# Five head pairs held to the program's order, copies moved behind maxima, and the first weight words on GpSimd's queue

## The chip, the cores and the metric

One core of a Trainium2 chip runs the whole program. The metric is the device time of one execution in microseconds; lower is better. TensorE (PE) multiplies into PSUM, VectorE (DVE) and ScalarE (ACT) read PSUM and work element by element, GpSimd (POOL) works on SBUF only. DMAs are issued from the queues of SyncE (SP), ScalarE and GpSimd.

## The reference: attention, then two feed-forward layers

```python
scores = scale * np.matmul(q, k.transpose(0, 1, 3, 2))      # q, k, v: 4 x 8 heads x 576 x 64
bias = -(cum[:, :, :, None] - cum[:, :, None, :])           # cum: running sum of max(s, 0)
scores = np.where(causal, -1000000000.0, scores + np.minimum(bias, 0.0))
scores = scores - np.max(scores, axis=-1, keepdims=True)
attn = np.exp(scores)
attn = attn / (np.sum(attn, axis=-1, keepdims=True) + 1e-09)
x = np.matmul(attn, v)                                      # then as 2304 tokens x 512
h = x @ w_in;  x = np.maximum(h, 0.0) ** 2 @ w_out          # 512 -> 2048 -> 512
h = x @ w2_in; return np.maximum(0.01 * h, h) @ w2_out      # once more, with a leaky ReLU
```

The weights arrive as 64-bit floats. The kernel takes them as pairs of 32-bit words and puts float32 values together from them.

## The kernel before

Attention runs in 16 pairs of heads. Each pair passes through seven slots, the pieces of `STEPS`: tiles of kind 0 (128 and 384 keys together), 2, 3 and 4 (the last 64 rows of both heads), for kinds 0, 2 and 3 once for each head of the pair. The loop in `attention` walks over slots y = 7x + st. In a slot it emits first the row maxima (`maxima`, VectorE) and the exponentials (`exponentials`, ScalarE, which also sums the rows into `sums`). Then come the TensorE instructions: transposes of a finished kind into PSUM (`flip`, two slots behind its exponentials), the product with v (`values`, for columns below 256 and above), and the scores of a kind to come (`scores`). `flip` also emits the copies of the transposed tiles out of PSUM into `pT` and `pX`: on ScalarE for kinds 0 and 2, on VectorE for kinds 3 and 4. PSUM has four `tr` banks for transposes and products, two `S` and two `h` banks for scores. Next come `gather` (product out of PSUM into `xo`), `inverse` (reciprocal of the sums on VectorE, spread over 64 columns by GpSimd into `ex`), `spread` (its transpose on TensorE) and `scale` (VectorE), each at a fixed slot count k0 after its pair began. For the first five pairs (`ALONE`, `PLAIN`) `scale` is done in two portions, columns 0 to 255 (a = 0) and the rest (a = 2).

Side work hangs on slots through `at_slot`: loads of q, k (`load_qk`), v (`load_v`, three buffers) and the bias rows (`load_bias`); `turn`, which transposes q and k on VectorE; `last_rows` on GpSimd; and `load_w`, which fetches one of the 16 column chunks of the first weight matrix (512 KB of words, `wst`, two buffers, on SyncE's queue) and three slots later has ScalarE (L114, L115), VectorE (L117, L120) and GpSimd (L122) put the words together, and then writes the chunk as a rounded part (ScalarE L169) and a rest (GpSimd L172). A chunk starts every two and a half slots from slot 11 on. From slot 35 on (`START[0]`) the matrix products of the first layer (`up1`) are filled in between attention's own TensorE work.

The order in which each engine gets its instructions is decided by a list scheduler with modelled times, except where `in_order` chains the instructions of an engine as they were written. Before, that chain covers TensorE from slot 35 on, and within single groups. Every engine then works through its queue strictly in that order. After attention two further layers follow in blocks of 768 tokens, mainly TensorE work.

Of the kernel before, what the change touches and what calls it, by code (L numbers as in the profile page):

```python
# [23 lines left out]
def attention_then_two_mlps(  # L24
# [24 lines left out]
    nc = tc.nc  # L49
# [108 lines left out]
    def load_w(fc, pool, stage, lo_engine=nc.gpsimd):  # L158

        st = stage.words()  # L160
        read_w(st, w1_in, fc, False)
        for _ in range(3):
            yield
        dst = pool.tile([P, 2, DM], F32R, tag=f"w{fc}", name=f"w{fc}")
        win[fc] = dst
        t = stage.word()
        yield from words(t, st)
        if fc < 10:
            nc.scalar.activation(dst[:, 0], f32(t), AF.Copy)  # L169
        else:  # L170
            nc.vector.tensor_copy(dst[:, 0], f32(t))
        lo_engine.tensor_tensor(dst[:, 1], f32(t), f32(dst[:, 0]), ALU.subtract)  # L172
# [193 lines left out]
    class Pair:  # L366


        def __init__(self, b, g, i):
            self.b, self.g, self.i = b, g, i  # L370
            self.h = [4 * g + 2 * e + i for e in range(2)]
            self.pT, self.sc, self.po = {}, {}, {}

# [142 lines left out]
    def flip(at, x, kind, ts):  # L516
# [19 lines left out]
        for r in range(2):  # L536
# [6 lines left out]
            else:  # L543
                jobs.append((p.pT[1][:, 1 - r, :, 2 * P:], src[:, 0, 0:4]))
                jobs.append((p.pX[:, r], src[:, 0, 4]))
        for out, src in jobs:
            if kind > 2:
                nc.vector.tensor_copy(out, src)
            else:
                nc.scalar.activation(out, src, AF.Copy)  # L550

# [119 lines left out]
    def attention(at, mg, mx):  # L671
# [65 lines left out]
        for x in range(len(pairs)):  # L737
# [8 lines left out]
            if x + 2 < len(pairs):  # L746
                if x and x % 2 == 0:
                    at_slot(y + 3, load_qk, at, x + 2)
                at_slot(y + 5, load_v, at, x + 2)

# [7 lines left out]
        for fc in range(FC):  # L758
            job = load_w(fc, wpool, stage)
            for gap in range(6):  # L760
                at_slot(CV + 5 * fc // 2 + (4 if fc > 7 else 0) + gap, step, job)
# [48 lines left out]
        for y in range(end + 14):  # L810
            x, st = divmod(y, n)
            if y == START[0]:
                fixed_from = len(nc.cur_bb.bb.instructions)
            if y < end:
                args = maxima(at, x, *STEPS[st])
                live[y] = args[0]
                behind = [args[-1], exponentials(*args[:-1])]
            fill(y, 0)
            tiled = len(nc.cur_bb.bb.instructions)
# [22 lines left out]
            for px in (x - 1, x):  # L842
# [8 lines left out]
                for when, a, b in portions:  # L851
                    if k0 == when:
                        scale(px, a, b)
                    if k0 == when - 4:
                        inverse(at, px, a, b)
                    if k0 == when - 1:
# [318 lines left out]
```

## Time and profile before

| | us |
|---|---|
| median of three runs | 930.9 |
| fastest run | 930.15 |
| profiled execution, its own time | 932.79 |
| its span, first to last instruction | 931.0 |
| TensorE busy | 898.3 (96%) |
| VectorE busy | 705.7 (76%) |
| ScalarE busy | 577.7 (62%) |
| GpSimd busy | 179.9 (19%) |

The profiled execution is 1.9 us above the median. Busy TensorE time is modelled for matmuls that overlap, so it tells where TensorE has work, not how well it is used. The mean granted clock of TensorE is 0.996 of full speed. Slots 0 to 34, the five pairs of the change, lie in the first 78 us of the span.

### The profile page before, as it was taken

How to read it: one execution, taken by the hardware profiler on the slowest of the kernel's cores; microseconds unless marked ns; L12 is line 12 of the kernel's file. 1: busy time of each engine (PE TensorE's matmuls, PEld its weight loads, DVE VectorE, ACT ScalarE, POOL GpSimd, SP SyncE). 2: the span in 40 equal slices, each digit the busy share in tenths (PEclk: the TensorE clock that was granted, in tenths of full speed). 3: DMA queues.
4: the chain of work that ended last, by engine and by line, in shares of the span. 5: the costliest groups of instructions: out<-in, count | busy, mean ns of one | idle time of the engine just before them, and what ended most of it. 6: DMA issues, size and time to landing. Idle time of an engine off the chain costs nothing.

```text
span 931.0 us, 16390 instructions
## 1 busy us (share of the span) xinstructions
PE 898.3 (96%) x5902; PEld 809.0 (87%) x5902; DVE 705.7 (76%) x1286; ACT 577.7 (62%) x1076; POOL 179.9 (19%) x290
## 2 busy tenths in 40 slices
PE   5878999999999999999999999999999999999997
PEld 3646777777777778999999999999999999999997
DVE  5888776876774267589897997787488697886964
ACT  4788876878886444365565556686577754444442
POOL 4357763344330001001112101001110000000000
PEclk9999999999999999999999999999999999999999
DMA  9776849778763377948649326668768575627303
GB/s 164 172 184 153 217 145 230 219 204 245 227 203 106 99 239 274 316 163 269 228 132 363 128 96 201 218 221 304 256 205 299 187 254 149 182 57 208 86 13 55
DMA packets 229569, 178.48 MB, mean 192 GB/s; under 512 B 139600, under 2 KB 206352, under 8 KB 229488
## 3 DMA queue, kind: packets, MB, share of 16 engines
q1 hardware_dynamic: 192568, 105.13, 41.7%
q10 hardware_dynamic: 27048, 38.16, 11.3%
q0 software_dynamic: 9872, 34.15, 10.5%
q8 instruction: 46, 0.75, 0.3%
q14 instruction: 35, 0.29, 0.1%
HBM read 111.25 MB, written 66.13 MB: 191 GB/s over the span
## 4 chain that ended last, share of the span: by engine, by line
PE 53%; issue 13%; DVE 6%; DMA 6%; POOL 1%; ACT 1%; POOLq 0%; ACTq 0%; DVEq 0%; SPq 0%
PE q L877 30%; PE h L661 16%; DVE op L984 3%; PE tr L569 2%; DMA gp<-gscr 2%; PE S L469 2%; PE tr L527 1%; PE S L457 1%; DMA gp<-qscr 1%; DMA wst<-in_moe_w_in_dram 1%; DMA qscr<-post 1%; DVE gp L978 1%; DMA wst<-in_moe_w_out_dram 1%; DVE wt L119 0%; POOL zscr L1046 0%
## 5 line engine op out<-in xcount | busy, mean ns | idle before, releaser
L877 PE MATMUL q<-op,w 128*128 128x384 f32 x3024 | 527.9, 335 | 4.0 <-DVE op L984 2.7
L877 PEld LDWEIGHTS q<-op,w 128*128 128x128 f32 x3024 | 523.7, 188 | 7.9 <-DVE op L984 5.0
L983 ACT ACTIVATE op<-gp 128x768 fp32r<-128x768 f32 x189 | 158.3, 846 | 152.3 <-PE q L877 128.4
L661 PE MATMUL h<-xs,w 128*128 128x512 f32 (+1 forms) x960 | 211.5, 374 | 1.2 <-ACT gs L640 0.8
L984 DVE TENSOR_TENSOR op<-gp,op 128x768 fp32r<-128x768 f32 x189 | 178.0, 953 | 40.6 <-ACT op L983 39.4
L661 PEld LDWEIGHTS h<-xs,w 128*128 128x128 f32 x960 | 163.6, 189 | 38.0 <-issue 6.0
L512 ACT ACTIVATE t<-t,m 128x256 f32<-128x256 f32 (+4 forms) x134 | 76.1, 569 | 44.1 <-DVE m L488 39.2
L488 DVE CUSTOM_DVE_ANT_0 t<-S,mask 128x128 f32<-128x128 f32 (+4 forms) x119 | 49.5, 460 | 43.3 <-PE S L469 28.2
L640 ACT ACTIVATE gs<-h 128x512 f32<-128x512 f32 (+1 forms) x80 | 43.8, 549 | 47.3 <-PE h L661 46.8
L185 POOL DMA_DIRECT2D wscr<-wt x48 | 26.6, 555 | 231.2 <-DVE wt L120 227.4
L950 DVE TENSOR_TENSOR post<-q,post 128x768 f32<-128x768 f32 (+1 forms) x55 | 51.6, 940 | 15.1 <-PE q L877 14.7
L469 PE MATMUL S<-Y 64*128 64x128 f32 (+3 forms) x324 | 42.9, 372 | 14.0 <-DVE Y L427 8.0
L930 ACT ACTIVATE post<-q 128x768 f32<-128x768 f32 (+1 forms) x56 | 43.8, 782 | 12.6 <-PE q L877 12.5
L114 ACT ACTIVATE wt<-wst 128x512 f32<-128x512 f32 x64 | 42.3, 661 | 12.2 <-DMA wst<-in_moe_w_in_dram 5.9
L569 PE MATMUL tr<-pT,v 128*64 128x320 f32 (+3 forms) x384 | 46.8, 387 | 2.5 <-ACT pT L550 2.0
L120 DVE SCALAR_TENSOR_TENSOR wt<-wst,wt 128x512 uint32<-128x512 uint32 x64 | 48.1, 753 | 0.9
L527 PEld LDWEIGHTS tr<-ident,t 64*128 64x128 f32 x720 | 28.6, 140 | 20.5 <-issue 11.3
L910 ACT ACTIVATE post<-post 128x768 f32<-128x768 f32 x36 | 30.4, 846 | 25.5 <-DVE post L950 25.4
L117 DVE TENSOR_SCALAR wt<-wt 128x512 uint32<-128x512 uint32 x64 | 31.7, 496 | 18.2 <-ACT wt L114 18.1
L569 PEld LDWEIGHTS tr<-pT,v 128*64 128x64 f32 x384 | 24.9, 137 | 23.1 <-issue 4.2
L115 ACT ACTIVATE wst<-wst 128x512 uint32<-128x512 uint32 x64 | 42.9, 670 | 2.7 <-DMA wst<-in_moe_w_out_dram 1.8
L198 DVE TENSOR_TENSOR w<-wq,w 128x512 fp32r<-128x512 f32 x49 | 33.3, 688 | 14.2 <-ACT w L197 13.9
(119 smaller groups left out, 943.7 us busy)
## 6 DMA issues: line engine op xcount, KB each, us to landing
gscr<-gs ACTq DMA_DIRECT2D x36, 512.0 KB
gp<-gscr SPq DMA_DIRECT2D x48, 384.0 KB
qscr<-post ACTq DMA_DIRECT2D x48, 384.0 KB
gp<-qscr SPq DMA_DIRECT2D x48, 384.0 KB
wscr<-wt POOLq DMA_DIRECT2D x48, 256.0 KB, 4.5
wst<-in_moe_w_in_dram SPq DMA_DIRECT2D x19, 512.0 KB
wst<-in_moe_w_out_dram SPq DMA_DIRECT2D x16, 512.0 KB
wst<-in_moe_w_out_dram POOLq DMA_DIRECT2D x16, 512.0 KB, 5.1
```

What stands on the lines that cost most here:

```text
L120: nc.vector.scalar_tensor_tensor(t, hw, 0xC0000000, t, ALU.bitwise_and, ALU.bitwise_or)
L469: nc.tensor.matmul(p.sc[kind][e][:, a:z], qs[hs, T * P:(T + 1) * P], ks[hs, :z - a], start=(n == 0 and y == 0), stop=(n == len(tiles) - 1 ...
L488: return nc.vector.tensor_tensor_reduce(t[:, a:z], sc, msk, -QK_SCALE, first, ALU.add, ALU.min, m).ins
L512: done = nc.scalar.activation(t[:, a:z], t[:, a:z], AF.Exp, bias=m[:, c:c + 1], scale=-1.0, accum_out=sums[:, s0:s0 + 1])
L569: p.anchor = nc.tensor.matmul(po[64 * e:64 * e + 64, a:n], p.vr[:, c, e], rhs[e], start=(y == 0), stop=(y == len(mm) - 1), skip_group_chec ...
L640: done = nc.scalar.activation(g, h[:, :w], AF.Relu)
L661: nc.tensor.matmul(h[:, :w], win[fc][:, a, c * P:(c + 1) * P], xs[j, c][:, z, :w], start=(c == 0 and y == 0), stop=(c == KC - 1 and y == 2))
L877: i = nc.tensor.matmul(*args, skip_group_check=True, **kw).ins
L930: done = nc.scalar.activation(t[:, xs], acc, AF.Copy)
L950: done = nc.vector.tensor_tensor(t[:, xs], acc, t[:, xs], ALU.add)
L983: a = nc.scalar.activation(t[:, 0], src, AF.Copy)
L984: c = nc.vector.tensor_tensor(t[:, 1], src, f32(t[:, 0]), ALU.subtract)
```

## The change

It changes orders and queues; every computing instruction stays, with its shape. The parts:

- From slot 0 to slot 34 VectorE and ScalarE, too, are chained in the order in which the program writes them, and TensorE's chain begins at slot 0 instead of 35.
- The VectorE copies of kinds 3 and 4 of pairs 0 to 3 are no longer written at the flip. They are kept and written in the next slot, behind that slot's maxima.
- `inverse` of the second portion moves from eight to nine slots after its pair began, and is put behind that slot's maxima.
- `load_v` moves by three slots, for all pairs.
- The words of the first weight matrix are fetched on GpSimd's queue instead of SyncE's (16 DMAs of 512 KB), and each chunk has one more slot between the addition on GpSimd and the rounded part.

```diff
     def load_w(fc, pool, stage, lo_engine=nc.gpsimd):
         st = stage.words()
-        read_w(st, w1_in, fc, False)
+        read_w(st, w1_in, fc, False, nc.gpsimd)
...
         yield from words(t, st)
+        yield
...
-        for out, src in jobs:
-            if kind > 2:
-                nc.vector.tensor_copy(out, src)
-            else:
-                nc.scalar.activation(out, src, AF.Copy)
+        def empty():
+            for out, src in jobs:
+                if kind > 2:
+                    nc.vector.tensor_copy(out, src)
+                else:
+                    nc.scalar.activation(out, src, AF.Copy)
+
+        if kind > 2 and x < PLAIN - 1:
+            p.empty.append(empty)
+        else:
+            empty()
...
-                at_slot(y + 5, load_v, at, x + 2)
+                at_slot(y + 8, load_v, at, x + 2)
...
-            for gap in range(6):
+            for gap in range(7):
...
+            if y == 0:
+                fixed_from = len(nc.cur_bb.bb.instructions)
             if y == START[0]:
-                fixed_from = len(nc.cur_bb.bb.instructions)
+                in_order(fixed_from, (nc.vector.engine, nc.scalar.engine))
             if y < end:
                 args = maxima(at, x, *STEPS[st])
                 live[y] = args[0]
                 behind = [args[-1], exponentials(*args[:-1])]
+            for p in pairs[max(0, x - 1):x + 1]:
+                while p.empty:
+                    p.empty.pop()()
...
-                    if k0 == when - 4:
-                        inverse(at, px, a, b)
+                    if k0 == (9 if a else when - 4):
+                        with after(behind[0] if a and y < end else None):
+                            inverse(at, px, a, b)
```

What the engines' queues hold at three places (line numbers after the change are its own):

**Place 1, ScalarE in pair 0.** Rows with `t,sums` or `Y,sums` are exponentials, `pT` rows the copies of transposed tiles (128x6x64 is kind 0, 128x2x3x64 kind 2). Before:

```order
L512 ACTIVATE t,sums<-t,m 128x384 x2
L512 ACTIVATE Y,sums<-Y,m 128x512
L550 ACTIVATE pT_244<-tr 128x6x64 x2
L512 ACTIVATE Y,sums<-Y,m 128x512
L512 ACTIVATE t,sums<-t,m 128x576
L579 ACTIVATE xo<-tr 128x256
L550 ACTIVATE pT_281<-tr 128x2x3x64 x2
```

After:

```order
L513 ACTIVATE t,sums<-t,m 128x384 x2
L552 ACTIVATE pT_244<-tr 128x6x64 x2
L513 ACTIVATE Y,sums<-Y,m 128x512 x2
L552 ACTIVATE pT_281<-tr 128x2x3x64 x2
L586 ACTIVATE xo<-tr 128x256
L513 ACTIVATE t,sums<-t,m 128x576
```

The kind 0 copies moved ahead of the first 512-wide exponential, the kind 2 copies ahead of the last exponential.

**Place 2, VectorE where pair 2 begins.** ISA rows are the maxima (the `m` rows store their result), `sums` rows are `inverse`. Before, the end of pair 1 and the first maxima of pair 2, and then what follows the four maxima of kind 0:

```order
L488 ISA t,m<-h,mask_77,m 128x288
L488 ISA m 128x1
L610 TENSOR_TENSOR xo<-xo,tr 128x256
L614 TENSOR_TENSOR xo<-xo,tr 64x64 x2
L585 TENSOR_SCALAR sums<-sums 128x5
L586 RECIPROCAL sums<-sums 128x5
L488 ISA t,m<-S,mask 128x128
```

```order
L117 TENSOR_SCALAR wt<-wt 128x512
L488 ISA t,m<-h,mask 128x384
L488 ISA m 128x1
L548 COPY pT_461<-tr 128x8x64 x2
L427 STREAM_TRANSPOSE Y<-kr 128x576
L548 COPY pT_461<-tr 128x4x64
L548 COPY pX<-tr 128x64
```

After, the same two stretches:

```order
L489 ISA t,m<-h,mask_77,m 128x288
L489 ISA m 128x1
L489 ISA t,m<-S,mask 128x128
L489 ISA m 128x1
L489 ISA t,m<-S,mask 128x256
```

```order
L550 COPY pT_461<-tr 128x8x64 x2
L117 TENSOR_SCALAR wt<-wt 128x512
L120 SCALAR_TENSOR_TENSOR wt<-wst,wt 128x512
L489 ISA t,m<-h,mask 128x384
L489 ISA m 128x1
L550 COPY pT_461<-tr 128x4x64
L550 COPY pX<-tr 128x64
L550 COPY pT_461<-tr 128x4x64
L550 COPY pX<-tr 128x64
L617 TENSOR_TENSOR xo<-xo,tr 128x256
L592 TENSOR_SCALAR sums<-sums 128x5
L593 RECIPROCAL sums<-sums 128x5
```

`inverse` of pair 1 moved from ahead of pair 2's maxima to behind the first maximum of kind 2; the kind 3 copies moved ahead of that maximum, and the transpose of k left the place between the copies of kinds 3 and 4.

**Place 3, GpSimd at the start of the program.** `v` is the padding of the first v tile, `wst` the words. Before:

```order
L330 AFFINE_SELECT ident<-ident 128x128
L406 MEMSET v 64x128
L331 AFFINE_SELECT mask<-mask 128x128
L348 MEMSET ag_88 4x576 x2
L360 DMA aug<-ka 32x2x576
```

After:

```order
L331 AFFINE_SELECT ident<-ident 128x128
L407 MEMSET v 64x128
L154 DMA wst<-in_moe_w_in_dram 128x4x256 x2
L332 AFFINE_SELECT mask<-mask 128x128
L349 MEMSET ag_88 4x576 x2
L361 DMA aug<-ka 32x2x576
```

The first two word loads, which wait for nothing, moved to the beginning of the program. Each later one stands behind the addition (L122) of the chunk two earlier.

## Rows read from the trace of the kernel before

**Rows 1.** Busy time of each engine by stretch, with TensorE's granted clock.
```profile
core 0: us, PE busy (x) PEld busy (x) DVE busy (x) ACT busy (x) POOL busy (x), PEclk, DMA share, GB/s
18.00:22.00 4.00, 4.00 (x35) 3.04 (x34) 0.36 (x2) 2.50 (x7) 0.00 (x0) 0.57 1.08 191
66.00:69.50 3.50, 3.45 (x13) 1.50 (x15) 3.50 (x10) 3.50 (x12) 0.33 (x1) 0.52 1.14 197
110.00:300.00 190.00, 189.82 (x1539) 144.87 (x1540) 135.11 (x377) 147.51 (x359) 73.03 (x113) 1.00 0.70 199
400.00:931.00 531.00, 522.71 (x2997) 518.67 (x2995) 427.59 (x543) 302.50 (x415) 41.49 (x68) 1.00 0.58 185
```

**Rows 2.** The same by pair, 0 to 4, cut at each pair's first maximum.
```profile
10.69:22.63 11.94, 9.44 (x76) 6.29 (x74) 6.31 (x27) 7.56 (x23) 2.45 (x10) 0.86 0.99 180
22.63:34.78 12.15, 10.75 (x123) 7.71 (x121) 9.35 (x36) 8.77 (x26) 2.36 (x9) 1.00 0.63 166
34.78:49.43 14.65, 11.83 (x135) 8.19 (x132) 12.89 (x43) 11.31 (x31) 8.06 (x12) 1.00 0.91 183
49.43:64.81 15.38, 10.89 (x113) 7.72 (x113) 13.57 (x42) 12.58 (x33) 9.59 (x13) 1.00 0.60 171
64.81:78.48 13.67, 10.92 (x98) 6.97 (x100) 13.61 (x41) 10.70 (x29) 7.51 (x9) 0.88 0.82 174
```

**Rows 3.** Waits of TensorE, 10 to 80 us: total, times, longest.
```profile
PE S L469 <- DVE m L488: 6.0, 4, 3.6
PE tr L527 <- DVE pX L548: 2.6, 3, 0.9
PE tr L569 <- ACT pT L550: 2.0, 1, 2.0
```

**Rows 4.** Waits of VectorE, the same stretch.
```profile
DVE sums L585 <- ACT t L512: 5.6, 5, 1.7
```

**Rows 5.** Timeline of ScalarE in pair 0: start, duration, instruction.
```profile
12.70 0.19 ACT L512 ACTIVATION_READ_ACCUMULATOR t<-t,m 128x1 f32 x1
16.22 0.72 ACT L512 ACTIVATE Y<-Y,m 128x512 f32<-128x512 f32 x1 [0.57 <-DVE m L488]
16.94 0.85 ACT L550 ACTIVATE pT<-tr 128x384 f32<-128x384 f32 x2
```

**Rows 6.** Timeline of TensorE: pair 0, and the same product in pair 1.
```profile
15.33 0.51 PE L457 MATMUL h<-ag,last 128*128 128x288 f32 x1
17.84 1.07 PE L569 MATMUL tr<-pT,v 128*64 128x256 f32 x8 [2.01 <-ACT pT L550]
31.23 0.87 PE L569 MATMUL tr<-pT,v 128*64 128x256 f32 x8
```

**Rows 7.** Timelines of VectorE and GpSimd, then groups from 34.78 to 80, and L585 to 90.
```profile
61.91 1.23 DVE L585 TENSOR_SCALAR sums<-sums 128x5 f32<-128x5 f32 x1 [1.71 <-ACT t L512]
61.84 2.50 POOL L172 TENSOR_TENSOR w<-wt,w 128x512 fp32r<-128x512 f32 x2
...
L585 DVE TENSOR_SCALAR sums<-sums 128x4 f32<-128x4 f32 (+1 forms) x6 | 4.6, 765 | 2.9 <-ACT t L512 2.9
L488 DVE CUSTOM_DVE_ANT_0 t<-h,mask 128x384 f32<-128x384 f32 (+1 forms) x9 | 4.6, 510 | 0.0
L585 DVE TENSOR_SCALAR sums<-sums x10: 127/272/1231, 12.9 to 79.6; 128x4 f32<-128x4 f32 x5, 128x5 f32<-128x5 f32 x5
```

**Rows 8.** Word loads that GpSimd issues in a later stage: issue ns, landing us.
```profile
L154 POOL DMA_DIRECT2D wst<-in_moe_w_in_dram x13: 753/753/763, 353.0 to 521.1; - x13
DMA to landing us min/median/max: 4.0/5.4/7.9
```

**Rows 9.** DMA queues, from 5 to 6 us and from 9 to 10 us: packets, MB, share.
```profile
q1 hardware_dynamic: 1252, 0.16, 98.4%
...
q0 software_dynamic: 49, 0.16, 61.9%
q1 hardware_dynamic: 693, 0.09, 55.9%
```

More of the change, by code (lines that the diff above doesn't have):

```diff
@@ L371, in __init__ @@
             self.h = [4 * g + 2 * e + i for e in range(2)]
-            self.pT, self.sc, self.po = {}, {}, {}
+            self.pT, self.sc, self.po, self.empty = {}, {}, {}, []
     pairs = [Pair(b, g, i) for b in range(B) for g in range(H // 4) for i in range(2)]
```

## The prediction

> **What bounds the kernel now.** I read three views in this order. First the busy time by stretch: from 110 to 300 us TensorE is busy 189.82 of 190 us, and from 400 to the end 522.71 of 531 [rows 1]. There the end is set by TensorE's own queue, and what comes earlier at 110 us should come earlier at the end. The change touches slots 0 to 34, the first 78 us, and only there does TensorE stand idle for long. The second view, the same by pair [rows 2], shows that pairs 0 to 4 take 11.94, 12.15, 14.65, 15.38 and 13.67 us. In pair 1 TensorE is busy 10.75 of 12.15 us. In pairs 2 to 4, where the weight words join in, VectorE is busy 12.89, 13.57 and 13.61 us: it is the engine nearest to its limit, with ScalarE behind it. The third view, the waits, says what the idle time was for. TensorE waited 6.0 us for maxima before it could write scores, once for 3.6 us, 2.6 us for the `pX` copies, and 2.0 us once for a `pT` copy on ScalarE [rows 3]. VectorE waited 5.6 us in five pieces at `inverse`, whose sums are finished only by the last exponential, while the next pair's maxima stood behind it [rows 4]. After two of the idle stretches TensorE's granted clock was low: 0.57 on the mean from 18 to 22 us and 0.52 from 66 to 69.5 us, so mostly at the 1.2 GHz level [rows 1].
>
> **The change, part by part.**
>
> *Pair 0.* TensorE waited 2.01 us, to 17.84, for the kind 0 copies [rows 6], which ScalarE began at 16.94, behind a 512-wide exponential that had itself waited for its maximum [rows 5]. After, they stand ahead of it. ScalarE is done with the kind 0 exponentials at 12.89 [rows 5]. Two exponentials of 384, at most 0.72 each (the duration of the wider one) and one copy pair of 0.85 bring the copies to 12.89 + 1.44 + 0.85 = 15.2. TensorE's kind 4 scores ahead of the product ended at 15.84 [rows 6] and come a little earlier, as the maxima that free their banks no longer stand behind `inverse`: I take 15.6. The product comes 2.24 us earlier. From product to the next pair's first maximum took 22.63 - 17.84 = 4.79 us at the low clock, but 34.78 - 31.23 = 3.55 us one pair later [rows 2, 6]. Without the idle stretch I expect the clock to stay up: 1.24 us more. Together -3.5. Bounds: -2.2 if the clock falls anyway; -4.5 if also the scores of kind 0, which now stand wholly ahead of those of kind 2, come 1 us earlier (an estimate: a quarter of the 3.55 us).
>
> *Pair 1.* Without the wait at `inverse` VectorE (9.35 us busy) is no limit; TensorE's 10.75 us are. Of the 1.40 us that it was not busy I leave 0.55 in: -0.85. Bounds 0 and -1.4.
>
> *Pairs 2 to 4.* VectorE's work is 12.89 + 13.57 + 13.61 = 40.07 us of 43.70 [rows 2]; the 3.63 us between are mostly waits at `inverse`, which now stands a slot later, behind a maximum. In return the kind 3 copies now stand right behind the four maxima of kind 0, and must wait until TensorE has written the scores of kind 2 and the transposes. I take 0.5 us in each pair, the length of the maximum that stood in this place before [rows 7]. 40.07 + 1.5 = 41.6: -2.1. Bounds: 0, if ScalarE, which the program's order now also holds and which was busy 11.31 and 12.58 us in pairs 2 and 3, waits at a word load or a copy for as long as VectorE did; and -7.4, if besides all 3.63 us the stretched instructions go. These are the small operations of `inverse`: 0.127 us at their shortest, but 1.23 us beside a GpSimd addition of 2.50 us for two; the six from 34.78 to 80 us take 4.6 us, 3.8 more than six short ones [rows 7]. The additions stay and the two engines meet as often, so I leave the stretching in. The Trainium skill, GPSIMD Engine Reference, section 8 (Key points), says that GpSimd shares its SBUF interfaces with VectorE and contends with some of its modes. The rows agree; by that rule stretching goes only where the two do not overlap, and the sum stays as it is, while with none left it would be 3.8 us lower.
>
> *Word loads on GpSimd.* An issue costs 0.753 us there [rows 8], 12 us for 16 of them over some 50 slots; GpSimd is busy 8.06, 9.59 and 7.51 us in pairs 2 to 4 [rows 2], which covers it; without that cover `ex` would come late and TensorE's `spread` with it. On SyncE's queue their waits vanish, and so does what stood behind them. Later v loads hide too: a tile is used 11 slots or more after its load, and its buffer is then free without waiting. Both 0. But the first two loads, 1.05 MB, now stand at the beginning of the program, beside q and k for pairs 0 to 2. Beside GpSimd's queue SyncE's moved 693 packets in a microsecond, alone 1252 [rows 9]. I expect pair 0's q and k to be mostly in before the words flow, and those of pairs 1 and 2 to have some slack. Bounds 0 and +4.2 us (1.05 MB at the 0.25 MB that the queues moved together in that microsecond [rows 9]). I take +0.5, near the lower end, since bytes moved forward are missing from the traffic later.
>
> *One more slot before the rounded part* costs nothing: the chunk is first used after slot 35.
>
> Sum: -3.5 - 0.85 - 2.1 + 0.5 = -5.95 us. It is made on an execution of 932.79 us, 1.9 above the median of the runs; I apply it to the median: 930.9 - 5.95 = **925.0 us**. The bounds add up to -13.3 and +2.0.
>
> **The rivals.**
>
> *Stretching goes too* (0.13). If maxima and GpSimd's additions fall apart in the new order, 3.8 us more: 921.2. For it: a wait of 3.6 us held one of the stretched ones [rows 3, 7]. Against it: VectorE and GpSimd have the same work as before.
>
> *The start pays in full* (0.13). The early words hold q and k up by the whole 4.2 us: 925.0 + 3.7 = 928.7. For it: SyncE's queue already fills the DMA engines at 98.4% at 5 us [rows 9].
>
> *The gain does not reach the end* (0.06). If a load of the later layers, rather than TensorE, sets their pace, the shift is absorbed: 930.9. Against it: their loads are released by TensorE's own progress.
>
> *ScalarE waits for words, and the kernel gets slower* (0.10). In program order ScalarE cannot pass the first instruction of a chunk whose words are not there. A load is issued behind the addition of the chunk two before, which leaves four slots, 4 x 41.6/21 = 7.9 us. Needed are one addition, 1.25 us [rows 7], the issue, 0.753, and the landing: 5.4 at the median, 7.9 at the longest [rows 8], so 7.4 or 9.9 us. At the longest, six chunks in pairs 2 to 4 wait 2.0 us each, 12.2 in all: 937.2. It decides from a landing of about 6.9 us on the mean, where 1.0 us a chunk eats the gain. Against it: the median fits. The Trainium skill, DMA: Bandwidth & Descriptors, section SWDGE vs HWDGE vs iDMA, speaks for it: GpSimd writes descriptors to SBUF that VectorE can lock it out of, while loads from SyncE and ScalarE are immune. The rows show no longer issue (753 to 763 ns at a busy VectorE), but a wide range of landings.
>
> **How the numbers follow.** The sum as it stands gets 0.58, with a range of its own from 921 to 928.5. From 917.5, near the sum of the lower bounds, to 931.5, which takes in the start and the lost shift, I leave out the slow rival (0.10) and some 0.05 below. Two per cent, about what a measurement of this kernel can tell from no change, is 18.6 us: that is more than all of TensorE's idle time in the five pairs, 13.96 us [rows 2], so below 912.3 gets 0.01; above 949.5 only a worse form of the slow rival, 0.02; the rest, 0.97, is within.
>
> **What would show it.** Right: pair 1's first maximum near 19 us instead of 22.63, no low clock from 18 to 22 us, no waits of VectorE at `inverse`, and pair 5's first maximum near 72.5 us instead of 78.48. Wrong: pair 0's first maximum later than 11.5 us, where it stands at 10.69 [rows 2]; ScalarE waiting for word loads by more than 6 us in all; or a gain at pair 5 that is gone at 300 us.

## The result, and the profile after

The changed kernel takes 942.3 us in the median of six runs (940.95 to 945.6), the kernel before 931.4 in six runs beside it, one of which, 1106.6, counts as slow and does not enter the ratio. The ratio is 1.0118, with a 95% interval from 1.0093 to 1.0144: it got slower by 1.2%. The profiled execution has 942.29 us and a span of 940.5; the span before was 931.0. So 9.5 us have to be found.

Busy time of each engine in the changed kernel, by pair, 0 to 4, cut at each pair's first maximum (columns as in [rows 1]; "PEclk" is TensorE's mean granted clock), to be read against [rows 2]:

```profile
core 0: us, PE busy (x) PEld busy (x) DVE busy (x) ACT busy (x) POOL busy (x), PEclk, DMA share, GB/s
13.30:21.43 8.13, 8.13 (x64) 5.04 (x62) 6.05 (x24) 6.38 (x22) 1.52 (x6) 1.00 0.94 162
21.43:31.84 10.41, 10.04 (x114) 7.08 (x111) 9.53 (x36) 7.54 (x25) 1.99 (x8) 1.00 0.54 111
31.84:48.59 16.75, 14.43 (x145) 10.19 (x143) 13.63 (x45) 13.23 (x35) 8.72 (x15) 0.90 0.88 187
48.59:64.53 15.94, 11.45 (x90) 7.67 (x89) 14.64 (x43) 11.87 (x31) 10.50 (x15) 0.91 0.57 156
64.53:85.27 20.74, 13.60 (x120) 9.33 (x118) 14.41 (x44) 14.41 (x38) 13.66 (x16) 0.75 0.74 161
```

The account in these rows: pair 0 begins 2.61 us later than before (13.30 against 10.69), pairs 0 and 1 are 3.81 and 1.74 us shorter (8.13 and 10.41 against 11.94 and 12.15), and pairs 2, 3 and 4 are 2.10, 0.56 and 7.07 us longer. That is 6.79 us late at pair 5's first maximum. At pair 15's it is 7.87, and behind it come another 1.6. The shift is carried to the end, since later on TensorE works through, as in [rows 1] (the second stretch ends 1.5 us behind the last instruction):

```profile
110.00:300.00 190.00, 189.36 (x1536) 144.57 (x1537) 140.76 (x385) 149.91 (x364) 82.85 (x122) 1.00 0.75 207
400.00:942.00 542.00, 529.69 (x3043) 525.74 (x3042) 433.41 (x551) 307.07 (x422) 41.61 (x68) 1.00 0.58 186
```

**The start.** The DMA queues of the changed kernel from 5 to 6 us (packets, MB, share of 16 engines; q0 is GpSimd's, q1 SyncE's):

```profile
q0 software_dynamic: 54, 0.22, 86.9%
q1 hardware_dynamic: 20, 0.00, 1.6%
```

In the same microsecond SyncE's queue had moved 1252 packets before [rows 9]. Now it moves 20, beside 54 large ones of the words. Its q and k stand behind them, and with them the bias rows `ag`, whose loads SyncE issues at 8.08 us instead of 6.08. TensorE waits for these rows last, as the timeline shows (start, duration, instruction, and in brackets the idle time before it and its releaser):

```profile
8.70 0.78 DVE L428 STREAM_TRANSPOSE Y<-qr 128x576 f32<-128x576 f32 x1 [1.54 <-DMA qr<-in_q_dram]
...
12.36 0.79 PE L470 MATMUL S<-ag 64*128 64x128 f32 x4 [1.17 <-DMA ag<-ka]
...
13.30 0.29 DVE L489 CUSTOM_DVE_ANT_0 t<-S,mask 128x128 f32<-128x128 f32 x1 [3.82 <-PE S L470]
```

**Pair 4.** Pair 5 is the first pair whose k and q pass through three engines: VectorE turns (L431), ScalarE rounds (L432), GpSimd takes the rest (L433). Before, the scheduler had VectorE turn them in the first 6 us of pair 4 (timeline of the kernel before):

```profile
66.40 0.77 DVE L430 STREAM_TRANSPOSE yt<-kr 128x576 f32<-128x576 f32 x1
...
70.00 0.77 DVE L430 STREAM_TRANSPOSE yt<-qr 128x576 f32<-128x576 f32 x1
```

In the program's order they stand in slots 31 and 32, in the second half. The changed kernel, timeline of all engines from 75 to 84 us:

```profile
75.36 0.63 ACT L624 ACTIVATE xs<-xh 128x512 fp32r<-128x512 f32 x1
...
76.03 0.69 DVE L625 TENSOR_TENSOR xs<-xh,xs 128x512 fp32r<-128x512 f32 x1 [2.11 <-ACT xs L624]
...
76.63 0.77 DVE L431 STREAM_TRANSPOSE yt<-kr 128x576 f32<-128x576 f32 x1
...
77.44 0.68 ACT L432 ACTIVATE Y<-yt 128x576 fp32r<-128x576 f32 x1 [1.45 <-DVE yt L431]
...
78.21 1.43 POOL L433 TENSOR_TENSOR Y<-yt,Y 128x576 fp32r<-128x576 f32 x1 [1.96 <-ACT Y L432]
...
80.31 0.58 PE L528 MATMUL tr<-ident,t 64*128 64x64 f32 x11 [3.08 <-ACT xo L586]
...
80.88 1.29 POOL L122 TENSOR_TENSOR wt<-wt,wst 128x512 uint32<-128x512 uint32 x1
...
82.13 1.40 POOL L433 TENSOR_TENSOR Y<-yt,Y 128x576 fp32r<-128x576 f32 x1
...
83.58 0.48 PE L470 MATMUL S<-Y 64*128 64x128 f32 x2 [1.69 <-POOL Y L433]
```

Read from top to bottom it is a chain from one engine to the next. VectorE stands at L625 until ScalarE has rounded the attention output (L624), with the turn of k behind it. ScalarE then waits for the turn, and GpSimd for ScalarE. TensorE waits 3.08 us for a copy that stands behind all this on ScalarE, and 1.69 us for the second rest, which on GpSimd stands behind an addition of the words (L122). The granted clock is low as well, ahead of this chain and from 82 us on, behind its waits (busy time by stretch, changed kernel):

```profile
62.00:64.00 2.00, 1.89 (x10) 1.34 (x7) 1.61 (x7) 2.00 (x6) 1.40 (x4) 0.50 0.65 144
64.00:66.00 2.00, 2.00 (x28) 1.79 (x25) 1.17 (x5) 2.00 (x7) 1.24 (x1) 0.50 0.96 247
66.00:68.00 2.00, 0.58 (x9) 0.40 (x5) 1.32 (x4) 0.65 (x3) 2.00 (x3) 0.50 1.20 234
68.00:70.00 2.00, 1.55 (x6) 0.84 (x6) 2.00 (x9) 1.92 (x6) 0.32 (x1) 0.50 0.76 147
...
82.00:84.00 2.00, 0.42 (x4) 0.42 (x6) 1.36 (x6) 1.64 (x6) 1.94 (x4) 0.54 0.56 127
84.00:86.00 2.00, 2.00 (x28) 1.90 (x26) 0.73 (x5) 1.28 (x5) 1.92 (x3) 0.50 0.48 113
```

0.50 is the 1.2 GHz level. Between the first maxima of pairs 2 and 6 the mean granted clock is 0.86 over 74.2 us, so 20.8 us lie at that level; before it was 0.97 over 64.9 us, or 3.9.

### The profile page after: what moved, and what is told of

It reads as the page before. It is cut to its first block, busy times and chain, and to the rows that moved or that the text cites. A ratio compares the mean times of both kernels' runs of the same rounds, so it can differ in the third digit from the quotient of the medians.

```text
span 940.5 us, 16389 instructions
## 1 busy us (share of the span) xinstructions
PE 903.4 (96%) x5902; PEld 812.9 (86%) x5902; DVE 710.1 (76%) x1286; ACT 577.2 (61%) x1076; POOL 191.4 (20%) x306
## 3 DMA queue, kind: packets, MB, share of 16 engines
q0 software_dynamic: 12176, 42.54, 13.4%
## 4 chain that ended last, share of the span: by engine, by line
PE 45%; issue 14%; DVE 6%; DMA 4%; POOL 2%; ACT 1%; ACTq 0%; POOLq 0%; DVEq 0%; SPq 0%
PE q L890 31%; PE h L668 11%; DVE op L997 3%; DMA gp<-gscr 1%; PE tr L576 1%; DVE gp L991 1%; PE S L470 1%; PE tr L528 1%; DMA zscr<-post 1%; DMA wst<-in_moe_w_out_dram 1%; POOL wscr L186 1%; POOL zscr L1059 1%; DVE gp L993 0%; DMA xh<-xscr 0%; PE S L458 0%
## 5 line engine op out<-in xcount | busy, mean ns | idle before, releaser
L963 DVE TENSOR_TENSOR post<-q,post 128x768 f32<-128x768 f32 (+1 forms) x55 | 51.6, 940 | 15.7 <-PE q L890 15.3
L470 PE MATMUL S<-Y 64*128 64x128 f32 (+3 forms) x324 | 42.9, 381 | 15.5 <-DVE Y L428 9.5
L114 ACT ACTIVATE wt<-wst 128x512 f32<-128x512 f32 x64 | 42.4, 663 | 16.9 <-DMA wst<-in_moe_w_out_dram 9.7
L943 ACT ACTIVATE post<-q 128x768 f32<-128x768 f32 (+1 forms) x56 | 43.8, 782 | 12.9 <-PE q L890 12.1
L117 DVE TENSOR_SCALAR wt<-wt 128x512 uint32<-128x512 uint32 x64 | 35.7, 558 | 21.1 <-ACT wt L114 20.9
L528 PEld LDWEIGHTS tr<-ident,t 64*128 64x128 f32 x720 | 29.0, 141 | 24.0 <-issue 12.5
L528 PE MATMUL tr<-ident,t 64*128 64x64 f32 x720 | 37.3, 234 | 8.2 <-ACT xo L586 4.1
L199 DVE TENSOR_TENSOR w<-wq,w 128x512 fp32r<-128x512 f32 x49 | 33.3, 687 | 14.3 <-ACT w L198 14.3
```

Of the source, the lines that this page charges most:

```text
L470: nc.tensor.matmul(p.sc[kind][e][:, a:z], qs[hs, T * P:(T + 1) * P], ks[hs, :z - a], start=(n == 0 and y == 0), stop=(n == len(tiles) - 1 ...
L528: nc.tensor.transpose(banks[r][:, 64 * n:64 * n + 64], t[hs, a:a + P], ident[hs, hs])
L943: done = nc.scalar.activation(t[:, xs], acc, AF.Copy)
L963: done = nc.vector.tensor_tensor(t[:, xs], acc, t[:, xs], ALU.add)
```

## The experiments

All of them against the kernel before, with runs of it on the same chip (its medians there: 931.7 to 932.2). The pair columns come from one profiled execution each. "Lead" is the first maximum of pair 5 and of pair 15 against the kernel before; minus is earlier.

| run | us | ratio, 95% | pair 0 starts | pairs 0 to 4 | lead at 5 | at 15 |
|---|---|---|---|---|---|---|
| before | 931.4 | | 10.69 | 11.9 12.2 14.7 15.4 13.7 | | |
| changed | 942.3 | 1.009-1.014 | 13.30 | 8.1 10.4 16.8 15.9 20.7 | 6.8 | 7.9 |
| 1 order to slot 27 | 937.3 | 1.003-1.007 | 13.53 | 7.7 10.4 14.4 15.4 17.4 | 0.4 | 2.1 |
| 2 words on SyncE | 938.1 | 1.005-1.008 | 10.64 | 8.2 10.7 16.2 17.6 21.2 | 6.0 | 5.3 |
| 3 before + order | 940.3 | 1.005-1.011 | 10.40 | 8.0 13.0 16.4 16.1 20.9 | 6.3 | 7.1 |
| 4 no order on two | 940.6 | 1.006-1.011 | 13.12 | 9.6 13.6 17.1 15.8 13.9 | 4.7 | 3.8 |
| 5 pairs 0, 1 alone | 934.9 | 1.002-1.005 | 10.37 | 8.1 12.6 15.1 16.2 16.4 | 0.3 | -2.2 |
| 6 TensorE's order | 933.8 | 1.001-1.004 | 10.68 | 9.5 12.1 17.2 14.3 16.2 | 1.5 | -0.9 |
| 7 rest of xs later | 941.9 | 1.010-1.014 | 13.51 | 7.6 10.4 14.4 16.7 20.6 | 4.7 | 8.6 |
| 8 order to 13, SyncE | 931.1 | 0.999-1.002 | 10.32 | 6.8 11.5 15.5 12.2 16.8 | -5.4 | -3.1 |
| 9 turn earlier | 937.3 | 1.002-1.007 | 13.61 | 7.5 10.4 14.5 16.3 18.5 | 2.3 | 1.6 |
| 10 7 and 9 | 938.0 | 1.004-1.009 | 13.07 | 8.4 10.4 16.6 15.9 18.8 | 4.7 | 4.4 |
| 11 7, 9 and 2 | 934.3 | 1.000-1.004 | 10.38 | 8.8 10.4 15.2 17.1 17.7 | 1.1 | 0.8 |
| 12 first words held | 942.7 | 1.006-1.014 | 10.69 | 7.0 15.7 15.1 15.9 21.1 | 7.0 | 7.9 |
| 13 idle time filled | 947.3 | 1.011-1.017 | 13.72 | 8.6 10.4 18.7 19.5 21.6 | 14.0 | 12.5 |
| 14 1 and 2 | 932.7 | 0.999-1.004 | 10.29 | 6.8 11.0 15.9 16.6 17.4 | -0.6 | -1.9 |
| 15 8, filled | 944.1 | 1.008-1.016 | 10.29 | 7.5 10.9 20.8 17.5 21.1 | 9.7 | 9.0 |
| 16 8, words on both | 933.1 | 1.000-1.004 | 11.11 | 8.0 10.4 15.2 13.4 16.7 | -3.7 | 0.4 |
| 17 14, words on both | 935.9 | 1.003-1.008 | 10.31 | 8.8 10.4 14.6 16.7 18.0 | 0.4 | 3.2 |
| 18 copies at the flip | 944.0 | 1.012-1.016 | 13.28 | 7.5 11.6 16.9 16.7 20.2 | 7.8 | 10.8 |

One execution is a narrow base for the end of a row: from pair 15's first maximum to the end the profiled executions take 643.1 to 648.5 us (before 644.1, changed 645.8), and no edit changes the program there. The times and ratios come from 4 to 10 runs each, and the profiled execution can lie well off their median: in experiment 2 it took 942.4 us, in 4 938.1, in 9 934.0.

### 1: the program's order ends at slot 27

```diff
-            if y == START[0]:
+            if y == START[0] - n:
                 in_order(fixed_from, (nc.vector.engine, nc.scalar.engine))
```

> The changed kernel, with VectorE and ScalarE held to the program's order in slots 0 to 27 alone; pair 4 (slots 28 to 34) is free again. In the changed kernel pair 4 took 20.74 us from its first maximum to pair 5's, against 13.67 before. Theory A, the program's order itself: from slot 28 on work that passes from ScalarE to VectorE and back (rounded parts of the attention output L624 to L625, the three steps of the turned k and q of pair 5, L431 to L433, the words L114 to L117) stands in both queues as written, and each engine waits for the other with the maxima behind it. Then pair 4 is near 14 us again and the time is 942.3 - 7.1 = 935.2. Theory B, GpSimd's queue: the words are fetched and added later than before, because loads and additions stand in one queue there, and that makes pairs 2 to 4 longer. Then pair 4 stays near 20 us and the time at 942.

937.3: 5.0 us less than the changed kernel, where A expected 7.1 and B nothing. Pair 4 takes 17.43 us, not 14, but VectorE no longer waits in it:

```profile
61.42:78.85 17.43, 13.52 (x137) 10.02 (x137) 17.30 (x46) 14.76 (x38) 12.73 (x17) 0.91 0.81 166
```

It is busy 17.30 of 17.43 us; in the changed kernel it was 14.41 of 20.74. So the order in slots 28 to 34 costs, as A says. About 3 of the 17.30 us are instructions that take longer than in the changed kernel: two L625 and two L592 take 5.23 us together, against 2.22 there, and each of them overlaps with a GpSimd instruction of 1.27 us or more, as in the stretching of [rows 7]. The longest of them (L625 takes 0.69 us at its shortest, above):

```profile
71.61 1.43 POOL L433 TENSOR_TENSOR Y<-yt,Y 128x576 fp32r<-128x576 f32 x1
71.75 1.84 DVE L625 TENSOR_TENSOR xs<-xh,xs 128x512 fp32r<-128x512 f32 x1
```

The run also showed something that neither theory had. Pair 2 lies ahead of the edit, where TensorE, VectorE, ScalarE and GpSimd have the same order as in the changed kernel, and yet it took 14.40 us instead of 16.75. The waits of TensorE and the product behind them, first in the changed kernel, then here:

```profile
36.97 0.56 PE L528 MATMUL tr<-ident,t 64*128 64x64 f32 x11 [1.39 <-DVE pX L550]
37.45 3.81 PE L576 MATMUL tr<-pT,v 128*64 128x320 f32 x16
```

```profile
36.79 0.56 PE L528 MATMUL tr<-ident,t 64*128 64x64 f32 x11 [1.39 <-DVE pX L550]
37.28 2.16 PE L576 MATMUL tr<-pT,v 128*64 128x320 f32 x16
```

The same wait of 1.39 us; behind it the same product takes 3.81 us in one execution and 2.16 in the other. The clock fell in the one and stayed up in the other.

### 2: the words back on SyncE's queue

```diff
-        read_w(st, w1_in, fc, False, nc.gpsimd)
+        read_w(st, w1_in, fc, False)
```

> The changed kernel, with the 16 word loads back on SyncE's queue, and all else as changed. Both theories: the two loads at the start of the program no longer lie beside q and k, so pair 0's first maximum is near 10.7 us again instead of 13.30, 2.6 us less. Theory A: nothing else is won, 942.3 - 2.6 = 939.7, pair 4 stays near 20 us. Theory B: pairs 2 and 4 shrink as well, by 2.1 and 7.1 us: 930.5.

938.1, 4.2 us less. Pair 0's first maximum is at 10.64, and of the lead at pair 15 the edit gives 2.6 us (7.9 to 5.3). Pairs 2 to 4 are no shorter: B falls. The 4.2 of the times exceed the 2.6 that this execution shows. It is the slowest of the ten, 942.38, and its stretch behind pair 15 is the longest of all (648.5).

### 3 and 4: the order alone, and all but the order

The first puts the two in_order lines of the change into the kernel before; the second takes the one for VectorE and ScalarE out of the changed kernel.

> The kernel before with one part of the change alone: the program's order on TensorE, VectorE and ScalarE for slots 0 to 34. Theory A: pairs 0 and 1 gain most of the 5.5 us that they gained in the changed kernel (perhaps less, as inverse stands ahead of the next maxima), pairs 2 to 4 lose at least the 9.2 us of pairs 2 and 4: 931.4 - 4 + 9.2 = 936.6. Theory B: the gain alone, 931.4 - 4 = 927.4.

> The changed kernel without the program's order on VectorE and ScalarE (the scheduler arranges these two again); TensorE stays held from slot 0. Theory A: no lockstep in pairs 2 to 4, and no gain in pair 0 either, while the start still costs 2.6 us: 931.4 + 2.6 = 934, and pair 4 near 14 us. Theory B: pair 4 near 20 us and a time of 940 or more.

The order alone makes the kernel before slower by 0.8%, 3.7 us more than A expected. It gives pair 0 its whole gain (7.99 us) and pair 4 its whole loss (20.94). Pair 1 is 13.02 us, so its gain needs the moved `inverse` and copies (experiment 18 parts the two). Without the order on the two engines pair 4 is 13.90 us, as A says, but the time, 940.6, is 6.6 above what A gave. The loss there lies in pairs 1 to 3, where the clock is low (pair 2 of that kernel: 0.80):

```profile
36.31:53.44 17.13, 13.20 (x119) 8.55 (x115) 14.16 (x42) 11.97 (x34) 8.70 (x12) 0.80 0.77 164
```

### 5, 6 and 8: the order for pairs 0 and 1 only

The fifth is the kernel before with the order of three engines for slots 0 to 13 and the copies and `inverse` of pair 0 moved; the sixth the kernel before with TensorE's order alone; the eighth the changed kernel with

```diff
-            if y == START[0]:
+            if y == 2 * n:
                 in_order(fixed_from, (nc.vector.engine, nc.scalar.engine))
```

and the words on SyncE's queue.

> The kernel before, with the change for pairs 0 and 1 alone: TensorE, VectorE and ScalarE held to the program's order in slots 0 to 13, the VectorE copies of pair 0 in the next slot, inverse of pair 0 a slot later behind the maximum. Slots 14 to 34 stay with the scheduler, the words stay on SyncE's queue, v and the extra slot stay as before. Theory A (the program's order pays in pairs 0 and 1 and costs in pairs 2 to 4): pair 2's first maximum 5.2 us earlier than before, as with the words back on SyncE's queue, and kept: 932.1 - 5.2 = 927. Rival C (the lead is lost in pairs 2 to 4 whatever holds their order, since VectorE is their limit and the words come at their own pace): the lead at pair 5's first maximum is 1 us or less, and the time 931 to 932.

> The kernel before, with TensorE alone held to the program's order from slot 0 on. Without the chain on VectorE and ScalarE the changed kernel still took 17.13 us for pair 2 (14.65 before) and the whole was 8.5 us longer than before, of which the start explains 2.4. Theory D, TensorE's chain is a cost of its own once the other two engines are arranged by the scheduler: pair 2 near 17 us, 935 or more. Otherwise (the rest comes from the later copies, inverse and v loads): 932.

> The changed kernel, with VectorE and ScalarE held in slots 0 to 13 alone and the words back on SyncE's queue; TensorE's chain from slot 0, the later copies, inverse and v loads of all pairs stay. Theory A: pairs 0 and 1 as in the changed kernel, without the 2.6 us of the start, and pairs 2 to 4 as before: 927. Theory D (TensorE's chain, or the later copies and inverse, cost in pairs 2 to 4 also without the other two chains): pair 2 near 17 us, 930 to 933.

The fifth is 4.1 us ahead at pair 1's first maximum and 0.3 behind at pair 5's: C was right on the lead, and the time, 934.9, is above both forecasts. The sixth, 933.8, lies between its two. TensorE's order alone gives pair 0 2.4 us and takes them back in pair 2, which needs 17.17 us, as D has it:

```profile
32.29:49.46 17.17, 14.75 (x145) 9.82 (x141) 13.34 (x42) 12.41 (x36) 8.67 (x14) 0.80 0.85 177
```

But the mean clock there is 0.80, and experiment 1 showed that one and the same order takes 16.75 or 14.40 us as the clock falls or not. So D is not shown by this execution. The eighth, 931.1, is the best of all and no faster than before. It is 8.5 us ahead at pair 4's first maximum, and has 3.1 of them left at pair 15's.

### 7, 9, 10 and 11: what makes pair 4 long

Edits of the seventh and of the ninth:

```diff
-        split([t[:, z] for z in range(2)], xf)
+        nc.scalar.activation(t[:, 0], xf, AF.Copy)
+        yield
+        nc.vector.tensor_tensor(t[:, 1], xf, f32(t[:, 0]), ALU.subtract)
```

```diff
-                late = 2 if x <= PLAIN else 0
+                late = 0 if x == PLAIN - 1 or x > PLAIN else 2
```

In the seventh the piece behind the `yield` is written two slots later.

> The changed kernel, with the rest of the rounded attention output (VectorE, L625) written two slots behind its rounded part (ScalarE, L624) instead of in the same slot. In the changed kernel VectorE waited there twice, 3.6 us in all, with maxima queued behind it. Theory A: without these waits pair 4 goes from 20.74 to about 16 us, a wait of 3.6 us and what the low clock adds behind it; the time 942.3 - 4.5 = 937.8. Rival C (VectorE waits elsewhere instead, since ScalarE is behind in any case): pair 4 stays above 19 us, 941 or more.

> The changed kernel, with the turned k and q of pair 5 written two slots earlier (slots 29 and 30 instead of 31 and 32). Pair 5 is the first whose k and q pass through three engines (VectorE turns, ScalarE rounds, GpSimd takes the rest). Where VectorE and ScalarE follow the program's order, all four kernels had the last rest end only 0.1 us ahead of pair 5's first scores on TensorE, which had waited 1.7 to 5.2 us for it; where the scheduler arranged them, the rests were done 3 to 5 us before. Theory E, the turn is written too late for three engines: pair 4 goes from 20.74 to 18 us, 942.3 - 3 = 939.5. Rival C (the scores only find another wait, since ScalarE and VectorE take turns in waiting): pair 4 at 20 us or more, 941 or more.

> The changed kernel with both edits in pair 4: the rest of the attention output written two slots behind its rounded part, and the turned k and q of pair 5 two slots earlier. With the first edit alone TensorE waited 5.2 us for the rest of k, and pair 4 took 20.60 us. Theory E: that wait goes, pair 4 takes 15.5 us, 941.9 - 5 = 937. Rival C: 19 us or more, 941.

> As the one with both edits in pair 4, and with the words back on SyncE's queue. Theory E: pair 2's first maximum 5.2 us earlier than in the kernel before, as measured with the words back; pairs 2 to 4 near 15, 16 and 15.5 us, 2.8 longer than before: 932 - 5.2 + 2.8 = 929.5. Rival C: 936.

The seventh, 941.9, refutes A in this form. VectorE's waits at L625 are gone, and pair 4 still takes 20.60 us, since another wait became the last one (timeline):

```profile
76.84 0.23 POOL L443 CAST last<-ag 4x64 fp32r<-4x64 f32 x1 [4.66 <-DMA ag<-aug]
...
81.50 1.22 PE L470 MATMUL S<-Y 64*128 64x128 f32 x8 [5.18 <-POOL Y L433]
```

GpSimd stood 4.66 us at bias rows that had not landed, with the rest of k behind them. The ninth was meant for that wait. The rests now run at 68.94 and 72.11 us and are done by 73.97, nearly 5 us before pair 5's first scores begin (78.71):

```profile
68.94 1.43 POOL L433 TENSOR_TENSOR Y<-yt,Y 128x576 fp32r<-128x576 f32 x1 [3.16 <-ACT Y L432]
...
72.11 1.86 POOL L433 TENSOR_TENSOR Y<-yt,Y 128x576 fp32r<-128x576 f32 x1
```

Pair 4 takes 18.48 us (18 expected) and the time is 937.3 (939.5 expected). E holds, though part of this execution's gain is pair 2, which met no low clock (14.48). With both edits the time is 938.0, near the 937 of E, but pair 4 is 18.76 and not 15.5: its clock is 0.68 on the mean. With the words on SyncE's queue it is 934.3, between E and C. What keeps pair 4 at about 18 us in the order is not one wait.

### 12: the first two word loads held back

```diff
+        if fc < 2:
+            tc.add_manual_dep(load, raw["rows"].name, ...)
```

> The changed kernel, with the words still on GpSimd's queue, but the first two loads held there behind the last rows of pair 1 instead of standing at the start of the program. It parts the start from the queue. If the start alone is what the words cost, pair 0's first maximum is near 10.6 us (13.30 in the changed kernel) and the time is that with the words on SyncE's queue, 938 (2.7 to 4.2 us less than 942.3). If GpSimd's queue costs as well, the first maximum is early, but pairs 2 and 3 are longer than with SyncE's queue, and the time is 940 or more.

Neither. Pair 0 starts at 10.69, and pair 1 takes 15.68 us instead of 10.41. The first load now lies at 15.7 us, beside q for pair 2, and the bias rows of pair 2, later on SyncE's queue, land late (timeline):

```profile
26.79 0.23 POOL L447 CAST last<-ag 4x64 fp32r<-4x64 f32 x1 [9.04 <-DMA ag<-aug]
...
28.99 0.44 PE L615 MATMUL tr<-ident,ex 128*128 128x128 f32 x2 [3.50 <-POOL ex L600]
```

GpSimd waits for these rows, `ex` stands behind them, and TensorE's `spread` waits for `ex`. The 1.05 MB cost something wherever they meet a load that is needed soon.

### 13 and 15: is it the clock?

```diff
+            if 2 * n <= y < 5 * n:
+                for z in range(2 if y < 3 * n else 3):
+                    nc.tensor.matmul(raw["spare"][z % 2][:, 3 * P:], ident, ident, start=True, stop=True, ...)
```

> The changed kernel, with added TensorE work that nobody uses: 56 products of 128x128 by 128x128, two in each of slots 14 to 20 and three in each of slots 21 to 34, into columns of the h banks that the scores leave free. They stand in TensorE's order ahead of transposes and scores that waited in the changed kernel. There the granted clock between pair 2's and pair 6's first maximum was 0.86 on the mean, 20.8 us at the lower level, against 3.9 before, and that stretch took 74.2 us against 64.9. Theory F, the clock: the idle stretches of 0.7 to 3 us cost more by the clock that falls behind them than by themselves; with them partly filled, less than 8 us are at the lower level, the stretch takes 69 us and the whole 937, although TensorE has some 11 us more to do. Theory A alone (the engines wait for each other, the clock of TensorE doesn't matter as it isn't the limit): the stretch stays at 74 us or grows, 942 to 947.

> The kernel with VectorE and ScalarE held in slots 0 to 13 and the words on SyncE's queue (931.1, 9.6 us at the lower clock between pair 2's and pair 6's first maximum, 68.5 us in all), with two such products in each of slots 14 to 34. Theory F: less than 4 us at the lower clock, the stretch takes 66 us, and the whole 929. Theory A alone: 931 or longer by what the 42 products add, up to 9 us.

The clock did stay up in the thirteenth, 0.96 on the mean, 6.3 us at the lower level:

```profile
32.69:111.61 78.92, 70.67 (x627) 51.81 (x626) 58.59 (x173) 55.63 (x141) 46.38 (x64) 0.96 0.57 139
```

But the stretch grew to 78.9 us, and both kernels are slower. F falls in this form. It isn't a clean test: the added products had a wait of their own (what TensorE idled for ahead of them),

```profile
its engine sat idle before it (us, times) until:
  DVE m L492: 15.6, 14
```

15.6 us for the maxima that read the other columns of the same bank, and TensorE was busy 70.7 us instead of 60.3. What the low clock costs by itself stays open.

### 14, 16 and 17: do the parts add up, and where does the lead go?

The fourteenth joins the edits of 1 and 2; 16 and 17 are 8 and 14 with the first four word loads on SyncE's queue and the others on GpSimd's.

> The changed kernel, with VectorE and ScalarE held in slots 0 to 27 and the words back on SyncE's queue: two edits that alone gave 5.0 and 4.2 us. If they add up, 942.3 - 9.2 = 933.1; if the start's 2.6 us are absorbed by what limits pairs 2 to 5, 936 to 937.

> The kernel with VectorE and ScalarE held in slots 0 to 13, with the first four word loads on SyncE's queue and the other twelve on GpSimd's. With all sixteen on SyncE's queue (931.1) it was 8.5 us ahead of the kernel before at pair 4's first maximum, 5.4 at pair 5's and 2.5 at pair 6's; in pair 5 SyncE's queue stood 5.7 us at a word load, with loads and stores of the attention behind it. Theory G, SyncE's queue gives the lead back: pair 5 takes 21 us instead of 24.0, the lead at pair 6 is 5 us and the time 928. Rival (the first layer sets the pace from pair 5 on): the lead at pair 6 is 2 to 3 us as before, 931.

> The kernel with VectorE and ScalarE held in slots 0 to 27, with the same split of the word loads. With all on SyncE's queue it took 932.7, and was 5.5 us ahead at pair 3's first maximum, 0.6 at pair 5's, 2.5 at pair 6's. Theory G: 930. Rival: 932 to 933, since its pairs 3 and 4 (16.6 and 17.4 us) lose to waits of VectorE and TensorE for each other, which no queue of loads decides.

The two parts add up: 932.7 against 933.1, the time of the kernel before. G falls: with SyncE's queue relieved, pair 5 takes 23.3 and 22.8 us, and the leads are gone all the same.

### 18: the copies at the flip again

```diff
-        if kind > 2 and x < PLAIN - 1:
+        if False:
```

> The changed kernel, with the VectorE copies of kinds 3 and 4 written at the flip again instead of behind the next slot's maxima; inverse stays behind the maximum. It prices the moved copies. By the prediction they cost 0.5 us in each of pairs 2 to 4 (a wait of VectorE for the transposes): without the move pairs 2 to 4 are 1.5 us shorter in all, pair 1 stays at 10.4, and the time is 941. If the moved copies are what makes pair 1 short (13.0 us with the program's order alone, 10.4 in the changed kernel), pair 1 is near 13 us and the time 944.

944.0, as in the second case, but pair 1 takes 11.62 us and not 13, against 10.41 in the changed kernel, and pairs 2 to 4 53.8 in all against 53.4. The moved copies bring 1.2 us in pair 1 and cost nothing in pairs 2 to 4. The ratios of the two kernels lie within each other's intervals, so the 1.7 us between their times are not clear of noise.

## Why the prediction was wrong

*Pair 0* (-3.5) was right in its sum, -3.81, but partly by luck: two sizes were off and cancel. The clock stayed at 1.00, as expected. The product with v came 1.49 us earlier, counted from the pair's first maximum (18.96 - 13.30 = 5.66 against 17.84 - 10.69 = 7.15), where 2.24 was forecast: TensorE, busy for the whole of the pair, came to it no sooner. From the product to the next pair's first maximum it took 2.47 us, not 3.55, about what the lower bound of -4.5 had allowed for scores of kind 0 that come earlier. In the changed kernel and in experiment 6 (TensorE's order alone):

```profile
18.96 0.87 PE L576 MATMUL tr<-pT,v 128*64 128x256 f32 x8
...
17.83 0.87 PE L569 MATMUL tr<-pT,v 128*64 128x256 f32 x8 [1.98 <-ACT pT L550]
```

In experiment 6 the wait for the copies is still there, 1.98 us, and pair 0 is 2.4 us shorter all the same: the clock stayed up behind it, and the next first maximum came 2.38 us after the product. So ScalarE's earlier copies, which the prediction priced highest, are worth the smaller part. Experiment 3 shows that the order of three engines alone gives the whole gain.

*Pair 1* (-0.85, at most -1.4) had the right sign and was too small: -1.74. Experiment 3 has 13.02 us with the order alone, experiment 18 11.62 with `inverse` moved too (and the words and v loads as changed), the changed kernel 10.41. The prediction saw only the wait at `inverse`; the moved copies were worth nearly as much (1.21 against 1.40), and it had put them down as a cost.

*Pairs 2 to 4* (-2.1, from 0 to -7.4) is the step that failed: +9.73. It took VectorE's busy time, 40.07 us, as the floor and added 0.5 us a pair for one new wait. VectorE is busy 42.68 us in the rows above, not far from that; but the three pairs last 53.43, so it idles 10.75. In the program's order an engine that can't go on holds up all that is behind it, and the prediction looked at one such place (the kind 3 copies, which cost nothing) and not at the work that goes from engine to engine in slots 28 to 34: L624 to L625, L431 to L432 to L433. That this part costs is shown by experiments 1 (5.0 us less) and 9 (the turn two slots earlier, 5.0 us less); in their profiled executions 3.3 and 2.3 us of it lie in pair 4, and 2.4 and 2.3 in pair 2, ahead of both edits, where the clock stayed up. Pair 2's own 2.10 us hang on that clock: with the same order it took 14.38 to 14.48 us in three executions, no more than the 14.65 before. The upper bound of 0 had no case in which the order itself is longer. The order from slot 28 on and the words' queue make up the whole net loss: with both undone the time is 932.7 us (experiment 14).

*The clock* was counted only as a gain in pair 0. The new waits of TensorE, 0.5 to 3.1 us each, came with 17 us more at 1.2 GHz. Its share of the loss is not parted from that of the waits.

*Word loads at the start* (+0.5, from 0 to +4.2): mis-sized. The term measured +2.61 in the trace and 4.2 us in the times of experiment 2. I had taken the shares of 9 to 10 us, where SyncE's queue keeps 693 packets [rows 9], for the start; there it keeps 20 of 1252. The Trainium skill, DMA: Bandwidth & Descriptors, section Queues, rings and completion order, says that a DMA engine takes whole packets from its queues in turn. By that rule large packets of words would take most of the time from small ones of q and k; the trace agrees in direction (54 packets carry 0.22 MB here, 1252 carried 0.16), and whether they go strictly in turn it can't show.

*Later word loads* (0) and *later v loads* (0): no harm was seen. These are ScalarE's largest waits from 32 to 112 us in the changed kernel, and none on that list is for words (total, times, longest):

```profile
ACT t L513 <- DVE m L489: 11.1, 10, 2.7
ACT t L513 <- DVE sums L592: 3.6, 1, 3.6
ACT Y L513 <- DVE m L489: 1.7, 2, 1.3
```

*The rivals.* "Slower" came true, at 942 and not 937, but not by its mechanism: the words landed after 5.2 us in the median and 8.0 at the longest, as in [rows 8], and ScalarE waited for maxima instead. The start paid 2.6 of its 4.2 us. The stretching did mostly go: the six L592 from pair 2 to pair 4 take 2.0 us, where their six took 4.6 before [rows 7], and nothing was won, as VectorE was no longer the limit. The shift reaches the end.

Of what was to show each step, pair 1's first maximum came at 21.43 instead of 19 and pair 0's at 13.30, later than the 11.5 named as the sign of an error; the low clock from 18 to 22 us and the waits at `inverse` in pairs 0 and 1 are gone as foretold. Pair 5's first maximum, 85.27 instead of 72.5, holds 12.8 of the 17.3 us by which the time was missed.

Two things stay open. Where the lead of pairs 0 and 1 goes in experiments 8, 14 and 16: pair 5 takes longer there in two of them (24.0 and 23.3 us against 21.2 before), and SyncE's queue is not why. And why experiment 4 is as slow as it is without any lockstep in pair 4, beyond its low clock in pairs 1 to 3.

## What to carry to other kernels

An order written out by hand can shorten a stretch (pairs 0 and 1 by 3.8 and 1.7 us), and costs where work passes from engine to engine within a few slots. Write each hand-over so early that its last engine is done a slot before the result is needed (experiment 9, 5.0 us). To hold only the stretch in which the gain was found is safer but need not pay: the lead of experiments 5 and 8 was mostly lost on the way, and they took 934.9 and 931.1 us against 932.1. The busy time of the busiest engine is no estimate for a stretch in which several engines follow a fixed order. A load that waits for nothing is issued at once, and 1 MB of it at the start stood in front of the loads on which everything waits: hold it back, but not into the next such load.

## What the runs showed of the hardware

The same wait of 1.39 us on TensorE, with the same order on four engines, let the clock fall in one execution (product 3.81 us) and not in another (2.16 us); pair 2 of that order took 16.75 and 16.59 us, or 14.40, 14.38 and 14.48. In pair 0 the clock fell behind a wait of 2.01 us in the kernel before and stayed up behind one of 1.98 us, ended by the same copies, in experiment 6. A single profile of a kernel with such gaps is good to about 2.4 us there. Keeping the clock up with work that nobody uses (0.96 instead of 0.86) made the kernel 5 us longer, not shorter, though that work brought waits of its own (experiment 13).

Two operations on VectorE took 1.84 and 1.20 us beside a GpSimd instruction in experiment 1 (L625, L592), where they take 0.69 and 0.17 at their shortest in the changed kernel.

Beside 54 packets of GpSimd's queue SyncE's got 20 packets through in a microsecond, where it moved 1252 alone in the kernel before; four microseconds later, beside 50, it moved 941. How the two share depends on more than their number.
